# Order of loads, a third output accumulator and new biases in a planned attention and gated-layer kernel

## The chip, the cores and the metric

The kernel runs on one core of a Trainium2 chip. The metric is the time of one execution in device microseconds; of several runs the median is given. The core has five engines that run side by side and wait for each other by semaphores: TensorE (PE, matrix products and transposes), VectorE (DVE), ScalarE (ACT), GpSimd (POOL) and SyncE (SP). In this kernel POOL and SP also issue nearly all transfers: POOL those that change the type from fp32 to bf16, SP those that transpose and the stores of the result.

## The reference

```python
# attention: 8 batches, 8 heads, 576 tokens, 64 columns; heads 0-3 plain, heads 4-7 dilated
scores = matmul(q, k^T) / 8
mask_plain = (rel >= 0) & (rel < 32)
mask_dil   = (rel >= 0) & (rel < 128) & (rel % 4 == 0)
x = softmax(where(mask, scores, -1e9)) @ v        # -> 4608 tokens x 512
# gated layer
h = x @ w_in                                      # 512 -> 2048
g = h * (1 / (1 + exp(-beta * h)))
out = g @ w_out                                   # 2048 -> 512, fp32
```

## The kernel before

All products are done in bf16. The work has two halves that are woven into each other.

**Attention**, per batch of 576 tokens. For heads 0 to 3 (the plain ones) keys are taken in blocks of 96 queries by 128 keys; for heads 4 to 7 (the dilated ones) the tokens are split by their remainder modulo 4 into four sets of 144, of which 128 are done as one block and the last 16 as a "tail". Steps by their names in the planner's lists: K and Q steps transpose keys and queries on PE (lines 474, 484) and copy them out of the accumulators; S are scores (688 dilated, 716 and 752 plain), T the tail's scores (657); each is followed by an exponential on ACT (624) and a multiplication by a 0/1 mask on DVE or POOL (628). V are the products with the values (793 dilated, 809 plain), U the tail's (778), each followed by a division by the row sum on DVE (643, 644). X and Y turn the result into xT, the transposed input of the gated layer (831, 846, 861).

Batches 0 to 2 (DIRECT = 3) load keys and queries to the buffers `st` by `direct_qk` and transpose them on PE. Batches 3 to 7 copy them to DRAM in bf16 by `cast` (POOL's queue) and read them back by transposing loads, `crossbar` (SP's queue, line 465). From batch 2 on (BY_DMA = 2) the result also goes to xT through DRAM and a transposing load (`back_dma`, lines 511 to 538), on SP's queue too. Values are loaded by `direct_vp` (plain, with a halo copied after the load) and by `direct_vd`, which makes three loads: one of the dilated values (line 439, later spread into `vd`) and two of the tail's values `vt_` (line 443).

**The gated layer** has nine tiles of 512 tokens. `slot_h` (line 892) makes one of 16 slots of 128 columns of h by four matmuls, then a tanh on ACT (901) and the gate on DVE (906). `block` makes one of four blocks of 128 rows of the output by 16 matmuls in four parts (927), scales it on ACT or DVE (942, 944) and stores it from SP (947). A part needs only four of the gated slots and its share of w_out; w_out comes in two loads, of which each serves two parts. The first four slots of the first tile (APART = 4) do the dilated half of x first, the plain half after it. Tile t needs attention of batch t and a part of the one before.

**The order** is written by a planner. Every step is a `plan.op` with the engines that can do it, an estimated time, its dependences and a due number `vt`. `Plan.run` keeps its own clock: of the steps that are ready it looks on each engine at those whose start, plus the step's bias, lies within NEAR (40 to 60 ns) of the earliest one, and takes the one with the smallest `vt`. The bias is `NUDGE[n]` in nanoseconds, where n counts the steps in the order in which they are made. So changing `vt` moves a step among others that are ready at the same time, and a bias makes a step look earlier or later than it is. For loads the planner keeps a clock for each queue, with an estimated rate and a latency, and lets at most eight be under way on one queue. Accumulator banks are taken by kinds with a limit each (CAPS): "o" is the kind of the output blocks of all tiles but the last, "h" of the slots, "s", "w", "a" of the attention, and there are eight banks in all. Where PE would stand idle in the plan before 80 us, the planner puts in a filler, a product of zeros (line 1040).

Due numbers of the loads: batch 0's keys and queries -9 to -8.97, its dilated values -8.5, its tail values (-8.5 + 1.255 + .001) -7.244, its plain values -8.4; w_in -7.3 to -7.28; the second batch's rows -7.25 to -7.22 and its values -7.2 to -7.19; w_out -7.2 and -7.19. From the fourth batch on, the loads of batch b are released together by a small copy on POOL (`t_pace`, line 1006), which waits until the work has come far enough; after it stand, by due number, the dilated key cast (b - 2), the dilated query cast (+.01), the plain key cast (+.02), the dilated and tail values (+.02 to +.022), the plain query cast (+.03) and the plain values (+.03).

## Time and profile before

| | before |
|---|---|
| median of 5 runs | 302.44 us (301.38 to 303.53) |
| the profiled execution | 301.85 us |
| its span, first to last instruction | 300.1 us |
| granted clock of TensorE, mean | 1.000 |
| busy share PE / DVE / ACT / POOL | 97% / 61% / 57% / 30% |
| matmuls of 512 columns with w_in (L892) | 550 recorded, 134.5 us |
| the same with w_out (L927) | 540 recorded, 134.1 us |
| fillers (L1040) | 65, the last at 45.0 us |
| transfers on POOL's queue | 18.58 MB, 59.2% of the span of the 16 DMA engines |
| transfers on the queues of SP and ACT | 22.95 MB, 37.4% |

The span is what the profile covers; the time of an execution is about 1.7 us longer. Times inside the profile count from the span's start. A row of the timeline gives the start, the length from the first start to the last end, the engine, the line, what is done (output <- inputs), how many instructions the row joins, and in brackets how long the engine sat idle and what ended that. Ends of matmuls are modelled, since they overlap, so the cost of a row is best read from its start to the next row's start. A POOL row of a transfer is the issue alone. A few per cent of the matmuls have no record.

### The profile page before, as it was taken

To read this page: it belongs to the slowest core of one execution; us is meant where nothing else is said; L and a number is where in the kernel's file an instruction comes from. 1 tells how busy PE (TensorE), PEld (TensorE's weight loads), DVE (VectorE), ACT (ScalarE), POOL (GpSimd) and SP (SyncE) were. 2 spreads that over 40 slices of the span, in tenths; PEclk is the share of its full clock that TensorE was granted. 3 is DMA by queue.
4 is the path that set the end of the run, shared out by engine and by line. 5 is a ranking of instruction groups with operands and counts; after the bars stand their busy time and mean duration, and the time that the engine had idled before them with its cause. 6 is when DMAs were issued, how large, how long until landed. Compare 5 with 4: busy or idle time off the path is not lost.

```text
span 300.1 us, 6040 instructions
## 1 busy us (share of the span) xinstructions
PE 292.6 (97%) x2304; PEld 150.2 (50%) x2342; DVE 184.3 (61%) x415; ACT 171.5 (57%) x311; POOL 90.6 (30%) x130
## 2 busy tenths in 40 slices
PE   7999999999999999999999999999999999999995
PEld 4765556445554445445444544455444444444454
DVE  4769778798858736886477745685781543443300
ACT  3868873867447644765585546764852654555311
POOL 8997363762155204600733065110000000000000
PEclk9999999999999999999999999999999999999999
DMA  7999999699979998999899979996024000100122
GB/s 164 189 210 203 206 190 205 96 174 192 215 152 176 155 146 212 180 151 222 146 191 154 195 158 174 164 202 156 0 75 115 36 36 35 37 35 35 60 82 70
DMA packets 111248, 41.98 MB, mean 140 GB/s; under 512 B 87620, under 2 KB 104596, under 8 KB 111220
## 3 DMA queue, kind: packets, MB, share of 16 engines
q0 software_dynamic: 60336, 18.58, 59.2%
q1 hardware_dynamic: 50740, 22.95, 37.4%
q8 instruction: 18, 0.29, 0.4%
q10 hardware_dynamic: 144, 0.07, 0.1%
q14 instruction: 10, 0.08, 0.1%
HBM read 37.76 MB, written 18.87 MB: 189 GB/s over the span
## 4 chain that ended last, share of the span: by engine, by line
PE 87%; DMA 8%; issue 1%; DVE 1%; POOL 1%; ACT 0%; DVEq 0%; POOLq 0%
PE bank L927 38%; PE bank L892 37%; DMA vp<-in_v_dram 7%; DMA st<-in_q_dram 2%; PE bank L1040 2%; PE bank L809 2%; PE bank L793 1%; PE bank L688 1%; PE bank L716 1%; PE bank L474 1%; PE bank L484 1%; PE bank L778 1%; PE bank L752 1%; PE bank L861 1%; ACT pt L624 0%
## 5 line engine op out<-in xcount | busy, mean ns | idle before, releaser
L901 ACT ACTIVATE tnh<-bank,beta_half 128x512 bf16<-128x512 f32 x144 | 98.1, 690 | 71.1 <-PE bank L892 64.2
L927 PE MATMUL bank<-w_out_bf,g 128*128 128x512 bf16 (+2 forms) x588 | 137.3, 367 | 1.4 <-issue 0.6
L906 DVE SCALAR_TENSOR_TENSOR g<-tnh,bank 128x512 bf16<-128x512 bf16 x144 | 97.2, 685 | 66.4 <-ACT tnh L901 65.8
L892 PE MATMUL bank<-xT,w_in_bf 128*128 128x512 bf16 (+1 forms) x566 | 136.1, 376 | 0.9
L892 PEld LDWEIGHTS <-w_in_bf 128*128 128x128 bf16 x584 | 55.4, 98 | 61.5
L927 PEld LDWEIGHTS <-g 128*128 128x128 bf16 x608 | 54.9, 98 | 56.2
L942 ACT ACTIVATE osb<-bank 128x512 f32<-128x512 f32 (+1 forms) x34 | 20.0, 590 | 31.6 <-PE bank L927 30.6
L624 ACT ACTIVATE pt<-bank 128x384 bf16<-128x384 f32 (+1 forms) x54 | 20.4, 463 | 5.3 <-PE bank L716 3.2
L624 ACT ACTIVATE ptd<-bank 128x512 bf16<-128x512 f32 x32 | 16.8, 603 | 3.7 <-PE bank L688 3.7
L644 DVE TENSOR_TENSOR xsp<-bank,rcp 96x384 bf16<-96x384 f32 x32 | 17.7, 554 | 1.1
L628 DVE TENSOR_TENSOR pt<-pt,mask_n 128x384 bf16<-128x384 bf16 (+1 forms) x39 | 13.4, 361 | 7.0 <-ACT pt L624 6.5
L643 DVE RECIPROCAL rcp<-bank 96x6 f32<-96x6 f32 (+2 forms) x72 | 12.9, 179 | 6.2 <-PE bank L809 3.0
L1006 POOL COPY pace<-xT 1x2 bf16<-1x2 bf16 x4 | 0.7, 176 | 50.1 <-DMA xT<-x 50.1
L399 POOL DMA_DIRECT2D vp<-in_v_dram x9 | 15.2, 1694 | 1.2 <-DMA vp<-in_v_dram 1.2
L644 DVE TENSOR_TENSOR xdm<-bank,rcp 128x256 bf16<-128x256 f32 x32 | 13.6, 424 | 1.1
L399 POOL DMA_DIRECT2D s<-in_q_dram x10 | 13.6, 1357 | 0.0
L628 DVE TENSOR_TENSOR ptd<-ptd,mask_d 128x512 bf16<-128x512 bf16 x27 | 10.8, 422 | 4.5 <-ACT ptd L624 3.8
L399 POOL DMA_DIRECT2D vt<-in_v_dram x16 | 13.3, 1000 | 0.0
L1040 PE MATMUL bank<-zero 128*128 128x256 bf16 x65 | 11.0, 314 | 1.1 <-DVE warm L307 1.1
L399 POOL DMA_DIRECT2D s<-in_k_dram x10 | 11.1, 1105 | 1.5 <-issue 1.1
L809 PEld LDWEIGHTS <-pt 128*128 128x128 bf16 x192 | 8.9, 97 | 5.1 <-issue 0.3
L944 DVE TENSOR_SCALAR osb<-bank 128x512 f32<-128x512 f32 (+2 forms) x4 | 2.1, 525 | 14.0 <-PE bank L927 14.0
(111 smaller groups left out, 184.3 us busy)
## 6 DMA issues: line engine op xcount, KB each, us to landing
out_dram<-osb SPq DMA_DIRECT2D x35, 256.0 KB, 2.6
s<-in_k_dram POOLq DMA_DIRECT2D x10, 288.0 KB, 7.2
s<-in_q_dram POOLq DMA_DIRECT2D x10, 288.0 KB, 9.5
w_out_bf<-in_moe_w_out_dram POOLq DMA_DIRECT2D x2, 1024.0 KB, 16.1
vp<-in_v_dram POOLq DMA_DIRECT2D x7, 288.0 KB, 15.8
st<-in_q_dram POOLq DMA_DIRECT2D x6, 288.0 KB, 12.6
x<-xsp SPq DMA_DIRECT2D x12, 144.0 KB
st<-in_k_dram POOLq DMA_DIRECT2D x5, 288.0 KB, 14.3
```

The source lines that it names most:

```text
L399: {"POOL": nc.gpsimd, "SP": nc.sync}[queue].dma_start(out=out, in_=in_)
L624: nc.scalar.activation(out=w(), in_=sc(), func=ACT.Exp, scale=SCALE)
L628: E[e].tensor_tensor(out=w(), in0=w(), in1=m(), op=ALU.mult)
L643: nc.vector.reciprocal(out=r, in_=p[..., D])
L644: nc.vector.tensor_tensor(out=dst, in0=p[..., 0:D], in1=r.unsqueeze(len(p.shape) - 1).to_broadcast(list(p.shape[:-1]) + [D]), op=ALU.mult)
L809: nc.tensor.matmul(pv[:, a, h2, :], lhsT=lhs, rhs=vp[kv][:, (2 * x + h2) * NI + 3 * j + a, 0:D + 1], start=True, stop=True)
L892: nc.tensor.matmul(bank(g)[:, a:z], lhsT=w_in_bf[:, kt, fb * P:(fb + 1) * P], rhs=xT[:, kt, xo + a:xo + z], start=(i == 0 and kt == kts[0] ...
L901: nc.scalar.activation(out=th[:, 0:n], in_=bank(g)[:, 0:n], func=ACT.Tanh, scale=beta_half[:, fb:fb + 1])
L906: nc.vector.scalar_tensor_tensor(out=g_t[t % 2][:, fb, c0:c0 + n], in0=th[:, 0:n], scalar=1.0, in1=bank(g)[:, 0:n], op0=ALU.add, op1=ALU.mult)
L927: nc.tensor.matmul(bank(g)[:, lo:hi], lhsT=g_t[t % 2][:, fb, tb * P:(tb + 1) * P], rhs=w_out_bf[:, fb, lo:hi], start=(fb == 0), stop=(fb = ...
L942: nc.scalar.mul(out=ob[:, lo:hi], in_=bank(g)[:, lo:hi], mul=0.5)
L1040: nc.tensor.matmul(BANKS[b][:, 0:256], lhsT=zero[:, 0:P], rhs=zero[:], start=True, stop=True)
```

## The change

It has five parts.

1. `direct_vd` of batch 0 gets -8.985 in place of -8.5, so its dilated values stand between the dilated queries (-8.99) and the plain keys (-8.98). The offset of its tail loads grows from 1.255 to 1.74, so that these stay where they were, at -7.244.
2. Both loads of w_out get -7.27 and -7.26: behind w_in, ahead of all rows of the second batch.
3. From the fourth batch on, the plain casts get .03 more (+.05 and +.06), so that they stand behind the dilated, tail and plain values.
4. The limit for kind "o" goes from 2 to 3 accumulators.
5. The table of biases is replaced: 29 entries between step 10 and step 1158 before, with sizes from 60 to 900; the new ones begin at step 48 and have sizes from 60 to 2500.

```diff
-    CAPS = {"h": 3, "p": 4, "o": 2, "z": 4, "a": 8, "s": 5, "w": 6}
+    CAPS = {"h": 3, "p": 4, "o": 3, "z": 4, "a": 8, "s": 5, "w": 6}
     SWITCH = 95
-    NUDGE = {10: 900, 16: -150, 32: -150, 34: 400, 40: -900, 65: -150, 99: -150, 121: -900, 159: -400,
...
+    NUDGE = {48: -900, 51: 150, 55: 150, 56: -150, 57: 400, 62: -2500, 63: -400, 70: -900, 73: 150,
+        75: -900, 78: 2500, 86: -400, 94: -150, 101: -2500, 118: 150, 126: -2500, 132: 900,
...
+        754: -2500, 767: 900, 774: -150, 926: -400, 941: -900, 1102: -900, 1119: -400, 1284: -60}
...
-            out.append(load("POOL", (vt_[b % 2][:, c, :, 0:D], src), list(tdeps), vt + (1.255 if b == 0 else .02 if b < DIRECT else 0) + .001 + .001 * c, 96, .2, lat=1100 if b < DIRECT else 4000))
+            out.append(load("POOL", (vt_[b % 2][:, c, :, 0:D], src), list(tdeps), vt + (1.7399999999999993 if b == 0 else .02 if b < DIRECT else 0) + .001 + .001 * c, 96, .2, lat=1100 if b < DIRECT else 4000))
...
-    ld[0]["vd"] = direct_vd(0, [], -8.5, [fill3])
+    ld[0]["vd"] = direct_vd(0, [], -8.985, [fill3])
...
-                 [], -7.2 + .01 * n, 2048, .41)
+                 [], -7.27 + .01 * n, 2048, .41)
         w_out_ld[2 * n] = w_out_ld[2 * n + 1] = o
...
-                c = cast(b, z, h0, [go], b - 2 + .01 * n)
+                c = cast(b, z, h0, [go], b - 2 + .01 * n + (0 if h0 else .03))
```

## The prediction

> **What bounds the kernel now.** I read the page's busy shares first, then its forty slices, then the costliest groups, and last the timeline of PE alone. The first two show one full engine:

> ```profile
> span 300.1 us, 6040 instructions
> PE 292.6 (97%) x2304; PEld 150.2 (50%) x2342; DVE 184.3 (61%) x415; ACT 171.5 (57%) x311; POOL 90.6 (30%) x130
> ...
> PE   7999999999999999999999999999999999999995
> ...
> PEclk9999999999999999999999999999999999999999
> DMA  7999999699979998999899979996024000100122
> ...
> L1040 PE MATMUL bank<-zero 128*128 128x256 bf16 x65 | 11.0, 314 | 1.1 <-DVE warm L307 1.1
> ```

> PE is full from the second slice to the last but one, always at the full granted clock; nothing else is over 61%. A 512-column matmul takes 0.216 us of it (0.86 us for four in the chain). So time goes away only where PE is busy with something useless, and it is added only where PE runs dry. The useless work is named in the last line: 65 fillers on zeros (L1040), which the planner emits where its own clock finds PE without work. The timeline of PE says when:

> ```profile
> 25.04 0.82 PE L1040 MATMUL bank<-zero 128*128 128x256 bf16 x6
> 25.69 1.03 PE L892 MATMUL bank<-xT,w_in_bf 128*128 128x512 bf16 x3
> ...
> 35.11 1.16 PE L1040 MATMUL bank<-zero 128*128 128x256 bf16 x9
> 36.20 0.43 PE L752 MATMUL bank<-qT,kT 64*128 64x96 bf16 x12
> 36.56 0.28 PE L1040 MATMUL bank<-zero 128*128 128x256 bf16 x1
> 36.68 1.89 PE L927 MATMUL bank<-w_out_bf,g 128*128 128x512 bf16 x7
> ...
> 44.99 0.27 PE L1040 MATMUL bank<-zero 128*128 128x256 bf16 x1
> 45.10 1.03 PE L927 MATMUL bank<-w_out_bf,g 128*128 128x512 bf16 x4
> ...
> 53.21 2.98 PE L892 MATMUL bank<-xT,w_in_bf 128*128 128x512 bf16 x12
> ```

> From start to start, the fillers after 26 us cost 36.20-35.11 = 1.09, 36.68-36.56 = 0.12 and 45.10-44.99 = 0.11: **1.32 us**. Those at 25.04 cost 0.65. All 48 others lie before 18.2 us, where the first product with w_in starts. After 45 us there are none, and PE's rows follow each other to the end: nothing downstream offers more than fractions.

> The break at 35 us ends in the first product with w_out (L927). Its transfers, from the timeline of POOL and from the view of that tile:

> ```profile
> 19.25 0.90 POOL L399 DMA_DIRECT2D w_out_bf<-in_moe_w_out_dram  x1
> 25.50 0.88 POOL L399 DMA_DIRECT2D w_out_bf<-in_moe_w_out_dram  x1 [0.40 <-DMA st<-in_k_dram]
> ```
> ```profile
> DMA to landing us min/median/max: 15.9/16.1/16.3
> ```

> They land at about 35.2 and 41.8. By then the 16 slots of the first token tile are through, so w_out is what is late.

> **The output weights first.** No transfer is added. One of 1,024 KB (1.05 MB) at the 206 GB/s of the window 30 to 37.5 takes 5.1 us. The last w_in lands at 10.96 + 12.8 = 23.8 (third issue in POOL's row at 9.45; page, DMA issues). With both parts of w_out next, they land at 28.9 and 34.0 instead of 35.2 and 41.8. PE's next work after 25.7 us is eight slots of the first tile, 32 x 0.216 = 6.9 us, to 32.6. From 28.9 on, first halves of output blocks can be taken too: with three accumulators 3 x 2 parts x 0.86 = 5.2 us, with two 3.4 us. Either bridges 32.6 to 34.0, when the second half is there; the third accumulator makes it safe. So I let the 1.32 us go. It cannot be more than 1.32 + 0.65; it is nothing if the planner finds other gaps.

> The 0.65 us at 25.04 I keep: there PE waits for the last part of w_in, which stands where it did. This is also why an earlier start would not help: before 25.7 PE can only do the first eight slots and batch 0's attention, and it had done both.

> The cost is that the second batch's rows, which lay ahead of one or both parts, go behind. The first key rows landed when the wait at 25.50 ended; they now land at 34.0 + 1.4 = 35.4 (288 KB at 206 GB/s), some 10 us later. The tail values of batch 0 move along; their product (PE at 27.93) is needed only by the second tile. The group's end does not move: the same bytes are in front of it, and batch 1's plain values (POOL idle 1.20 at 44.33 for a vp landing) arrive near 43.5 as before. On POOL each issue blocks until the eighth before it has landed; batch 1's dilated values then issue at 28.9, its plain ones at 34.0, and batch 2's keys after batch 1's last key transposes, near 40 instead of 29 to 32. The queue still holds batch 1's values until 44, so this is hidden by 4 us; if that cover goes, batch 2's rows slide by what is missing.

> What batch 1's attention loses is room. DVE and ACT now have this to do:

> ```profile
> 26.00:36.00 10.00, 9.90 (x161) 5.83 (x161) 8.20 (x16) 8.33 (x17) 5.23 (x7) 1.00 1.26 206
> 36.00:53.20 17.20, 16.88 (x243) 9.92 (x244) 13.67 (x36) 10.44 (x25) 8.30 (x13) 1.00 1.57 201
> 53.20:72.00 18.80, 18.64 (x164) 9.36 (x155) 15.57 (x37) 13.90 (x28) 11.89 (x15) 1.00 1.33 139
> ```

> (Columns after the length: busy PE, weight loads, DVE, ACT, POOL; clock; DMA share; GB/s.) In the first two rows DVE and ACT do 40.6 us. Eight slots take 8 x (0.69 + 0.69) = 11.0 of it; the remaining 29.6, nearly all of batches 1 and 2, must now start after about 36.6 (35.4 and the transposes). Up to 53.2 that is 16.6 us on each engine, 33.2 in all: 89% busy. In the third row, the fullest stretch, they reach 29.5/37.6 = 78%; at that rate the work ends at 36.6 + 29.6/(2 x 0.78) = 55.6. What covers it is output work: the L927 rows from 36.7 to 53.2 hold 41 matmuls of the tile's 64, so some 23, or 5.0 us, are left. PE, 1.3 us ahead, therefore has work until 53.2 - 1.3 + 5.0 = 56.9. The chain by itself is no longer: the last query rows at 40.2, transposed, copied, scored, exponentiated and masked in about 5 us by the rows from 34.7 to 38.6, meet the values at 46, where L809 starts now (45.96). I take 0. The bounds are 0 and a stall of 3.5 us (if the pair reached only 65%: 36.6 + 22.8 = 59.4, against 56.9, and a last link of 1 us).

> The TensorE clock stays at 1.00 in every row above, and there is no idle stretch of PE that could tell what one costs. [...]

> **The other parts.** Batch 0's dilated values move ahead of its plain keys and queries: 256 KB at the 189 GB/s of that stretch, so those come 1.4 us later and the values 2.9 us earlier. The dilated halves of the first slots can begin at the first w_in, which removes fillers before 18 us, but the wall at 25.7 stands: 0, between -2.2 (the wall is partly the planner's own estimate: w_in landed at 23.8, and 0.3 more) and +1.4. Mask, identity and issue order on POOL change without bias by some 0.3 us each, under the queue's backlog: 0.

> From the fourth batch on, the plain casts go behind all values. POOL issues the same eight transfers; the plain query cast lands later by the plain values' time, and the plain values earlier by the two casts. SP, which issues the transposing loads in order, then meets batch b's plain ones later. The tightest case:

> ```profile
> 107.90 3.27 SPq L465 DMA_TRANSPOSE qT<-s  x1
> ...
> 111.32 0.48 DVE L248 COPY vp<-vp 32x1280 bf16<-32x1280 bf16 x1 [1.17 <-DMA vp<-in_v_dram]
> ...
> 116.49 0.69 PE L716 MATMUL bank<-qT,kT 64*128 64x96 bf16 x24
> ```

> The transposing load would start about 111.3 - 107.9 = 3.4 us later and the scores near 120. PE does w_out and w_in products in that time, and the back transposes of batch 3, which stood in SP's queue behind this load, come sooner. In the other batches the scores (L716 at 84.8, 154.9, 190.6, 206.5) start 9 us and more after that load's issue. I take 0; bounds -0.5 and +2.

> Biases: they reorder about equal work on a full PE. Rows 'issue' ahead of L927 sum to 0.6 us on the page; -0.6 to +1.5, I take 0.

> **Sum.** -1.3 us. The profiled execution took 301.85 with a span of 300.1, so 298.8 and 300.5; against the median of the runs (302.44, from 301.38 to 303.53) it is 301.1. I forecast between the two: **300.8**.

> **Rivals.**
> - *The start gets shorter too* (the wall at 25.7 is the planner's; -2 to -4.2, 298.2 to 300.4, say 299.2). For: w_in landed at 23.8 and PE took it at 25.69. Against: its place in the queue is unchanged. Chance 0.2.
> - *The fillers only move* (to the wall, or to 50 to 56 us before the second tile): 301.7 to 303.1, say 302.4. For: the planner's estimate makes them. Chance 0.17.
> - *DVE and ACT become the bound from 36 to 57 us*: the second batch's transposed rows are late, PE has used up the first tile's output blocks, and waits. From 56.9 on every microsecond is paid; 3.5 of stall less 1.3 gives +2.2, 304.2 and up to 306 where batch 2 slides as well. For: 89% needed against 78% seen. Against: 5 us of output work in reserve. Chance 0.16.
> - The forecast itself, 299.9 to 301.7: 0.47.

> Differences under 0.5% (1.5 us) can't be told from none here: 300.9 and 304.0 are the limits. Of the forecast's 0.47, 0.30 lies below 300.9. Faster 0.30 + 0.20 = 0.50; the same 0.17 + 0.17 = 0.34; slower 0.16. The range leaves out most of the slower case and the best end of the first rival: 298.5 to 304.0.

> **What would show it.** Right: both w_out issues ahead of all second-batch rows, landing near 29 and 34; no L1040 row after 26 us; the first L927 row at 29 to 34; the second tile's L892 stream starting near 52; DVE and ACT nearly full from 37 to 54. Wrong: L1040 rows or PE idle for ACT or DVE between 46 and 58, PE idle anywhere after 100 us for a qT load, or a first w_in product well before 18.2 together with the slots done before 25.

## The result and the profile after

The changed kernel takes 303.34 us (median of 48 executions, 301.66 to 306.34), the kernel before beside it 302.03 us (88 executions, 300.87 to 303.53). The ratio is 1.0037, with a 95% interval from 1.0027 to 1.0048; a ratio here is one of means, without executions over 1.5% above the fastest of their kernel (one of the 48). So the change made the kernel slower by 0.37%, some 1.1 us, or 1.3 us by the medians, where I had forecast 1.6 us less than the median of 302.44 then shown; it is less than a few runs could tell from none, but these many do. The times alone held a clue. They lie in three groups with gaps between them: 18 from 301.7 to 302.8, 26 from 303.1 to 304.3, and 4 from 305.8 to 306.3. The kernel before has one broad group.

The first profile of the changed kernel fell into the lowest group (302.58 us) and shows almost nothing wrong. Lines are shifted by 8: L892, L927 and L1040 are now L900, L935 and L1048. The page:

```profile
span 300.6 us, 6020 instructions
PE 291.7 (97%) x2294; PEld 149.4 (50%) x2333; DVE 183.9 (61%) x418; ACT 169.9 (57%) x304; POOL 95.2 (32%) x134
...
L1048 PE MATMUL bank<-zero 128*128 128x256 bf16 x56 | 10.8, 328 | 1.3 <-DVE warm L315 1.1
```

There are nine fillers fewer, yet their busy time is 10.8 us against 11.0, and seven still stand after 26 us, where none was expected. The timeline of PE says where they are now:

```profile
24.13 0.71 PE L1048 MATMUL bank<-zero 128*128 128x256 bf16 x5
25.64 2.15 PE L900 MATMUL bank<-xT,w_in_bf 128*128 128x512 bf16 x9 [0.80 <-DMA w_in_bf<-in_moe_w_in_dram]
...
30.09 0.38 PE L1048 MATMUL bank<-zero 128*128 128x256 bf16 x2
...
31.17 1.03 PE L935 MATMUL bank<-w_out_bf,g 128*128 128x512 bf16 x4
...
57.92 2.33 PE L900 MATMUL bank<-xT,w_in_bf 128*128 128x512 bf16 x9
```

The first product with w_out comes at 31.17 instead of 36.68, and after 30.30 there is no filler at all. The second tile's stream, however, begins at 57.92 instead of 53.21, while the first tile's output blocks fill PE up to there. Summed from start to next start, the fillers compare like this:

| stretch, us | before | changed, first profile | changed, three more profiles |
|---|---|---|---|
| 0 to 6.6 | 4.28 | 5.29 | 5.07 to 5.21 |
| 6.6 to 18.2 | 3.99 | 3.20 | 3.20 |
| 18.2 to 26 | 0.66 | 1.51 | 0.60 to 0.61 |
| from 26 | 1.32 | 0.77 | 0.96 |
| all | 10.24 | 10.77 | 9.84 to 9.98 |

The 1.51 of the first profile holds the wait of 0.80 us for w_in. So the fillers mostly moved: 0.4 to 0.6 us went after 26 us, and the sum ends 0.3 to 0.4 us below that of before, or 0.5 us above it with the wait. Against that stands a new wait: near 6.3 us PE stands dry for 0.55 to 1.29 us in these four profiles (under 0.4 in the kernel before), for the constant `add_d` that POOL makes for the scores. POOL ends it at 6.37 us in the first profile instead of 5.37, behind the moved load of batch 0's dilated values. That goes far to explain why a good execution is no better than the kernel before. It does not explain the two upper groups.

A second profiled execution did (run "again" below, the same kernel, 305.88 us). SP's timeline of it, ahead of the place where PE runs dry:

```profile
159.45 1.97 SPq L519 DMA_DIRECT2D x<-xsp  x2
168.33 1.28 SPq L473 DMA_TRANSPOSE kT<-s  x1
...
170.32 1.31 SPq L473 DMA_TRANSPOSE qT<-s  x1
171.73 3.26 SPq L546 DMA_TRANSPOSE xT<-x  x2
```

and PE's timeline in the same execution:

```profile
173.62 1.03 PE L935 MATMUL bank<-w_out_bf,g 128*128 128x512 bf16 x4
177.03 5.31 PE L900 MATMUL bank<-xT,w_in_bf 128*128 128x512 bf16 x16 [2.38 <-DMA xT<-x]
```

SP has issued the writes of batch 5's result to DRAM at 159.45 and 161.01; by the trace they have landed at 167.85 and 168.76, and the back transposes (xT, L546) could follow. But the two transposing loads of batch 6's plain keys and queries (kT, qT, L473) stand ahead of them in SP's order, and these wait for casts that land at 168.28 and 170.09. The back transposes go out at 171.73 and 173.22, the first of them 3.9 us after its source was there. The last output block ready is used up at 174.65, the data of the first back transpose land at 176.98, and PE stands idle for 2.38 us. Then 16 matmuls take 5.31 us, where the first profile has 3.62 for the same 16:

```profile
175.43 3.62 PE L900 MATMUL bank<-xT,w_in_bf 128*128 128x512 bf16 x16
```

The views by stretch of the stalled execution say why; their columns are those of the prediction:

```profile
177.00:180.00 3.00, 2.97 (x9) 1.13 (x10) 0.69 (x1) 0.69 (x1) 1.72 (x4) 0.59 0.66 135
180.00:181.00 1.00, 1.00 (x4) 0.38 (x3) 0.06 (x1) 0.69 (x1) 1.00 (x3) 0.51 0.57 41
181.00:184.00 3.00, 3.00 (x15) 1.35 (x14) 2.01 (x3) 1.97 (x3) 3.00 (x5) 1.00 1.03 181
```

The granted clock fell to half, from 177.57 us for 3.41 us by the trace, and PE lost another 1.7 us. In the kernel before, SP has the same instructions in this order:

```profile
157.26 2.63 SPq L465 DMA_TRANSPOSE kT<-s  x1
...
162.97 2.32 SPq L465 DMA_TRANSPOSE qT<-s  x1
165.38 0.53 SPq L511 DMA_DIRECT2D x<-xsp  x1
168.78 1.29 SPq L538 DMA_TRANSPOSE xT<-x  x1
...
171.30 1.30 SPq L538 DMA_TRANSPOSE xT<-x  x1
```

and PE this row:

```profile
174.12 2.75 PE L892 MATMUL bank<-xT,w_in_bf 128*128 128x512 bf16 x11
```

There qT is also ahead of xT, but it is gone by 165.3, before the result is written: the two writes land at 168.76 and 171.29, and each back transpose follows its write at once. What PE takes at 174.12, with no wait, is the data of the first one, which land at 172.33. So this place had 1.8 us to spare before the change, and the change took that away.

Where do the late casts come from? In the first profile after, batch 6's transfers are released at 147.64, 3.3 us later than before (144.35). The plain key cast lands 19.1 us after the release and the query cast 21.9 us (before: 10.8 and 18.6), because all the values are now issued ahead of both. So kT is later by 8.3 us and qT by 3.3 us through the third part, and both by another 3.3 us through the release. The release waits for the second back transpose of batch 4, which lands at 147.01 instead of 143.73. That one too stands behind batch 5's plain loads, issued at 136.46 and 139.89 when their casts have landed (before: 127.08 and 133.09). So part of the later release comes by the same way, one batch earlier; how much is not shown. With 3.3 us alone the query cast would have landed near 166.3 us (estimate, 162.96 + 3.3), ahead of the writes that the back transposes wait for. By that it took both delays.

### The profile page after: what moved, and what is told of

Same layout as the page of the kernel before. It is cut to its first block, busy times and chain, and to the rows that moved or that the text cites. A ratio compares the mean times of both kernels' runs of the same rounds, so it can differ in the third digit from the quotient of the medians.

```text
span 300.6 us, 6020 instructions
## 1 busy us (share of the span) xinstructions
PE 291.7 (97%) x2294; PEld 149.4 (50%) x2333; DVE 183.9 (61%) x418; ACT 169.9 (57%) x304; POOL 95.2 (32%) x134
## 4 chain that ended last, share of the span: by engine, by line
PE 89%; DMA 4%; POOL 3%; issue 2%; DVE 0%; ACT 0%; POOLq 0%; DVEq 0%
PE bank L935 41%; PE bank L900 39%; DMA w_in_bf<-in_moe_w_in_dram 4%; PE bank L817 2%; PE bank L696 1%; PE bank L801 1%; PE bank L724 1%; PE bank L482 1%; PE bank L786 1%; PE bank L492 1%; POOL st L407 0%; POOL w_in_bf L407 0%; PE bank L760 0%; PE bank L665 0%; POOL vp L407 0%
## 5 line engine op out<-in xcount | busy, mean ns | idle before, releaser
L935 PE MATMUL bank<-w_out_bf,g 128*128 128x512 bf16 (+2 forms) x581 | 137.8, 367 | 1.8 <-issue 0.6
L900 PE MATMUL bank<-xT,w_in_bf 128*128 128x512 bf16 (+1 forms) x572 | 136.7, 376 | 1.5 <-DMA w_in_bf<-in_moe_w_in_dram 0.8
L900 PEld LDWEIGHTS <-w_in_bf 128*128 128x128 bf16 x584 | 55.8, 98 | 63.7 <-DMA w_in_bf<-in_moe_w_in_dram 1.1
L935 PEld LDWEIGHTS <-g 128*128 128x128 bf16 x608 | 54.5, 98 | 55.4
L950 ACT ACTIVATE osb<-bank 128x512 f32<-128x512 f32 (+2 forms) x30 | 17.4, 581 | 22.0 <-PE bank L935 21.7
L632 ACT ACTIVATE pt<-bank 128x384 bf16<-128x384 f32 (+1 forms) x54 | 21.1, 461 | 10.8 <-PE bank L724 7.6
L651 DVE RECIPROCAL rcp<-bank 128x4 f32<-128x4 f32 (+2 forms) x72 | 12.9, 179 | 9.0 <-PE bank L801 3.6
L636 POOL TENSOR_TENSOR pt<-pt,mask_n 128x288 bf16<-128x288 bf16 (+1 forms) x10 | 7.4, 762 | 32.2 <-ACT pt L632 16.4
L636 DVE TENSOR_TENSOR pt<-pt,mask_n 128x384 bf16<-128x384 bf16 (+1 forms) x36 | 11.7, 352 | 9.1 <-ACT pt L632 8.9
L952 DVE TENSOR_SCALAR osb<-bank 128x512 f32<-128x512 f32 (+1 forms) x8 | 5.1, 636 | 13.7 <-PE bank L935 13.7
L1048 PE MATMUL bank<-zero 128*128 128x256 bf16 x56 | 10.8, 328 | 1.3 <-DVE warm L315 1.1
L407 POOL DMA_DIRECT2D vp<-in_v_dram x9 | 10.2, 1130 | 4.1 <-DMA w_out_bf<-in_moe_w_out_dram 4.1
## 6 DMA issues: line engine op xcount, KB each, us to landing
s<-in_q_dram POOLq DMA_DIRECT2D x10, 288.0 KB, 10.2
```

What stands on the lines that cost most here:

```text
L407: {"POOL": nc.gpsimd, "SP": nc.sync}[queue].dma_start(out=out, in_=in_)
L632: nc.scalar.activation(out=w(), in_=sc(), func=ACT.Exp, scale=SCALE)
L636: E[e].tensor_tensor(out=w(), in0=w(), in1=m(), op=ALU.mult)
L651: nc.vector.reciprocal(out=r, in_=p[..., D])
L900: nc.tensor.matmul(bank(g)[:, a:z], lhsT=w_in_bf[:, kt, fb * P:(fb + 1) * P], rhs=xT[:, kt, xo + a:xo + z], start=(i == 0 and kt == kts[0] ...
L935: nc.tensor.matmul(bank(g)[:, lo:hi], lhsT=g_t[t % 2][:, fb, tb * P:(tb + 1) * P], rhs=w_out_bf[:, fb, lo:hi], start=(fb == 0), stop=(fb = ...
```

## The experiments

I went in with theory A (the start: w_in lands just when it is needed), theory B (the crowded second batch) and theory C (the clock is at half for longer at the start). Theory D, the queue of SP in batch 6, was formed on the second profile; F is what A to C become beside it. In the later expectations "rival C" means something else, full transfer engines, and R and S are named where they come up.

**The changed kernel again.** No edit.

> The changed kernel once more, for a second profile and its spread beside the variants. Theory A (the start): the 48 times lie in groups near 302.1, 303.6 and 306.1 us because the last part of w_in now lands just when PE needs it (25.59 against 25.64 us; before it landed 23.8 and was used at 25.69), so that any delay of that transfer goes straight to the end. In a profile whose span is over 301.3 the first product after the wall near 25.6 us then starts up to 1.6 us later, and all else is shifted by that. Theory B (the crowded second batch): the first slots start at 25.6 as in the first profile, and a long span gains its time between 36 and 60 us, where batch 1's attention is crowded. Theory C (the clock): a long span shows the TensorE clock at half for longer at the start (over 5.8 us).

Measured: 303.16 us (301.80 to 306.48), ratio 1.0038 [1.0011, 1.0065]. The profile is the one shown above. It speaks against theory A: w_in's last part lands at 24.47 and is taken at 24.54 without a wait, while the wait of 0.80 us for it, with a landing at 25.59, is in the first profile, of the lowest group.

**The tail mask behind the loads of w_in, in the changed kernel.** One bias is put back; only POOL's order changes, and the last part of w_in lands at 24.33 us. In the first profile of the changed kernel that was 25.59, but in the three others it is 24.47 to 24.65, so the edit moves less than it was meant to.

```diff
-    NUDGE = {48: -900, 51: 150,
+    NUDGE = {10: 900, 48: -900, 51: 150,
```

> The changed kernel with the old bias of step 10 alone (+900): the tail mask goes on POOL behind the issues of w_in instead of between the first and the second. Every other engine keeps its order. Theory A: w_in's second and third parts are issued 1.1 us sooner, the third lands near 24.5 instead of 25.6, the 0.8 us that PE waits there go and the group near 303.6 becomes rare: 0.8 to 1.5 us faster than the changed kernel, equal to the kernel before or up to 0.4 us faster. Theory B: w_in may land earlier, but the time stays within 0.3 us of the changed kernel's.

Measured: 302.99 us (301.70 to 306.51), ratio 1.0019 [0.9999, 1.0038]. The groups stay: five executions from 301.7 to 302.6, six from 303.0 to 304.4, one at 306.5. Nothing changes that can be told apart. With w_in landing early and without a wait in all three profiles from the upper groups (again, again_2, again_3), theory A falls.

**The reverse, in the kernel before.** Its bias on step 10 is taken away, so the tail mask goes between the loads of w_in; again only POOL's order changes, and w_in's last part lands at 24.10 instead of 23.80.

```diff
-    NUDGE = {10: 900, 16: -150,
+    NUDGE = {16: -150,
```

> The kernel before without the bias of step 10: the tail mask goes ahead on POOL, between issues of w_in, and no other engine changes its order. Theory A: w_in's last part lands about 1 us later, at 24.8 instead of 23.8, still ahead of its use at 25.69, so the time stays within 0.5 us, slower if anything (up to 0.5 us) because the reserve is down from 1.9 to 0.9 us. Theory B: no change.

Measured: 301.37 us (300.92 to 302.87), ratio 0.9981 [0.9964, 0.9998], the wrong way for A. It was run again later (the expectation calls the tail mask the dilated one):

> The kernel before without its bias on step 10, once more (only POOL's order changes: the dilated mask is built among the loads of the input weights). If its first ratio, 0.9981, stands: 0.996 to 0.9995. If it was chance: 0.999 to 1.002.

Measured: 302.25 us (301.26 to 303.03), ratio 1.0010 [0.9992, 1.0028]. The gain did not stand, and the order at the start is worth nothing measurable in either kernel.

**The old biases with the four other parts.** The table of the kernel before in the changed kernel.

> The changed kernel with the old table of biases: its four other parts without the fifth. Theory A: the mask and the identity return behind and ahead of w_in, so w_in lands 1 us or more sooner; as fast as the kernel before or up to 1.5 us faster. Theory B: the second batch's rows are as late as in the changed kernel, so it is 1 us or more slower than the kernel before. Against both: the old biases were numbered for another order, and PE may run dry anywhere, which would show as idle time of PE after 60 us.

Measured: 310.59 us (308.56 to 310.87), ratio 1.0257 [1.0231, 1.0283]. The fillers after 26 us take 4.9 us instead of 0.8 to 1.0, and PE stands dry before 97.5, 120.9 and 222.5 us for 0.9, 1.7 and 0.9 us. The new biases are worth 7 us to the new order.

**The two plain loads behind the back transposes, from the fifth batch on.** The plan stays. When it comes to such a load before batch b - 1 has its two back transposes, the load is put aside and issued right behind them. Only SP's order changes.

```diff
+        if not h0 and b > DIRECT:
+            o.after = b - 1
```

> The changed kernel with one thing altered: on SP the transposing loads of plain queries and keys of the fifth batch on are issued behind the back transposes of the batch before them, instead of ahead of them; every other engine's order is as in the changed kernel. Theory D (the later plain casts make those loads wait in SP's queue, the back transposes stand behind them, the stored output blocks run out, and in many executions PE stands dry near 174 us or at the same place in another batch, up to 2.4 us and then 3.4 us at half clock): no execution near 306, no group at 303 to 304.4, median 301.7 to 302.3, ratio to before 0.998 to 1.001, PE never idle for 0.5 us after 26 us. Theory F (the stall at 174 us is rare and by itself; the 303.6 group is made elsewhere, at the start or in the second batch): only the times at 306 go, median still near 303, ratio near 1.003. Rival: the plain loads that are now late make the batch's own score work late, ratio above 1.004.

Measured: 302.29 us (301.64 to 309.60), ratio 1.0003 [0.9977, 1.0029] over the eight executions below 307. Seven executions lie from 301.6 to 302.5, none from 303.0 to 304.4, but five from 304.9 to 309.6. The profile, from the lower group, has no PE wait of 0.5 us after 26 us. D's group is gone and something new has come. In the batches on either side, the plain keys and queries now stand last, the queries 3.6 to 4.7 us ahead of their scores.

**The same in batch 6 alone.**

```diff
-        if not h0 and b > DIRECT:
+        if not h0 and b == 6:
```

> The changed kernel with batch 6's two plain transposing loads alone issued on SP behind batch 5's back transposes; every other order on every engine stays. It is the earlier experiment cut down to the batch in which the stall was seen. Theory D: no stall near 174 us, no execution at 303.0 to 304.4, median 301.7 to 302.3; and the executions at 304.9 to 309.6 that the wider experiment had in 5 of 12 are gone, since they came from the other batches' loads, whose data the scores need 3 to 5 us after they landed there. If they stay, this batch's own loads or a transfer nobody reordered make them. Rival C (full DMA engines): executions near 303.5 and 306 stay.

Measured: 301.95 us, and all 11 executions between 301.61 and 302.67; ratio 1.0016 [1.0007, 1.0026]. SP's timeline, with lines shifted once more (kT and qT are L490, xT is L566):

```profile
159.41 2.12 SPq L539 DMA_DIRECT2D x<-xsp  x2
162.55 0.36 SPq L976 DMA_DIRECT2D out_dram<-osb  x1
167.97 3.04 SPq L566 DMA_TRANSPOSE xT<-x  x2
171.11 1.30 SPq L490 DMA_TRANSPOSE kT<-s  x1
172.51 1.32 SPq L490 DMA_TRANSPOSE qT<-s  x1
```

and PE's at the place of the stall:

```profile
173.86 1.03 PE L956 MATMUL bank<-w_out_bf,g 128*128 128x512 bf16 x4
174.73 3.62 PE L921 MATMUL bank<-xT,w_in_bf 128*128 128x512 bf16 x16
```

The casts land at 167.92 and 170.99 here, the query cast later than in the stalled execution, and it does no harm. The upper groups are gone, and so are the executions above 304.9 of the wider edit, which therefore came from the other batches' loads. Which one of those loads it was is not shown. SP is idle from 162.9 to 167.97, and what the first back transpose waits for there is its write, issued at 159.41 and landed at 167.91. So transfers set that time, as in the stalled execution (167.85), and the order added 3.9 us to it there. Of that wait rival C may have a share; that busy DMA engines make these writes take over 8 us is not shown, for the kernel before has a lower DMA share from 165 to 170 (1.14 in the view by stretch, against 1.64 here) and its first write takes 7.4 us.

To see whether anything else was lost, the changed kernel and this version were run side by side on one chip.

> The changed kernel once more, beside the next run on the same chip. Theory D alone: 302 to 303.4 median, with executions near 302.1, near 303.5 and near 306. Nothing new is expected of it; it is the measure for the next one.

> The changed kernel with batch 6's two plain transposing loads behind batch 5's back transposes, once more, beside the changed kernel. Theory D alone (all the loss is the stall near 174 us): no execution above 303.0, median 1.0 to 1.5 us below the changed kernel's median on this chip, and level with the kernel before, ratio 0.998 to 1.0015. Theory S (something at the start is lost as well, some 0.5 us): the same step down from the changed kernel, but ratio 1.001 to 1.003 to the kernel before.

Measured: the changed kernel 303.54 us (301.94 to 306.27), ratio 1.0058 [1.0034, 1.0083]; with the two loads moved 302.01 us (301.66 to 302.36), ratio 0.9996 [0.9981, 1.0011]. The places of two instructions on one queue are worth 1.5 us. Here that is the whole loss and theory S is not needed; the earlier run of the same version, 1.0016 [1.0007, 1.0026], leaves some 0.5 us. Whether anything of that size is lost besides stays open.

**A second profile of the changed kernel between the groups.**

> The changed kernel once more, for a second profile and more executions. Theory D: again three groups of times near 302.1, 303.6 and 306.1; the profile's time says which: near 303.6 or 306 it holds a PE wait of 0.5 us or more for an xT transpose after 100 us, near 302.1 it holds none. Theory F: near 303.6 the profile holds no such wait, and the loss stands before 60 us.

Measured: 303.35 us (301.66 to 303.72), ratio 1.0023 [1.0002, 1.0043]. The profiled execution took 303.45 us and has one PE wait of 0.5 us after 26 us, 1.39 us for xT before 176.28; the profiled execution of the run just before (again_3) took 303.73 us and waits 1.63 us at the same place:

```profile
176.28 3.63 PE L900 MATMUL bank<-xT,w_in_bf 128*128 128x512 bf16 x16 [1.39 <-DMA xT<-x]
176.56 3.63 PE L900 MATMUL bank<-xT,w_in_bf 128*128 128x512 bf16 x16 [1.63 <-DMA xT<-x]
```

In neither did the clock fall there. So each group has its cause in a profile: no wait near 302; 1.4 to 1.6 us of wait near 303.5; 2.4 us of wait and 1.7 us of half clock near 306. Of all 84 executions of the changed kernel 28, 47 and 9 are in the three groups, and none lies between 304.3 and 305.6. The mean clock, which is on record for every execution, bears this out: 0.993 or 0.994 in all nine of the highest group, as 3.41 us at half clock would give, and at least 0.998 in the 75 others. The kernel before is not quite free of such a fall: beside the variants two of its 96 executions took 306.3 and 306.6 us with a clock of 0.994. Theory C finds nothing: the first record of full clock begins at 5.76 us in the first profile (ahead of it fillers start 0.21 us apart, later 0.11) and at 6.90, 4.10 and 5.38 us in the three from the upper groups.

**The third part alone in the kernel before**, with the old biases.

> The kernel before with only the third part, the values' casts ahead of the plain ones from the fourth batch on, and the old biases. Theory D: the plain transposing loads' casts land 4 to 8 us later and the back transposes behind them too, so PE stands dry in some batches: 302.8 to 306, ratio 1.002 to 1.013, with a PE wait on an xT transpose in the profile. Theory F (the start and the second batch make the loss): level with before, ratio 0.999 to 1.001.

Measured: 306.36 us (304.25 to 307.51), ratio 1.0125 [1.0090, 1.0161]. After 26 us PE waits once, 3.4 us before 113.61, for the second back transpose of batch 3, issued at 103.92, and the clock is at half for 3.41 us behind it. No load that waits for its cast holds this one; ahead of it SP has only the issues of the first (3.74 us) and of the dilated queries (3.49 us). Its own data take 9.65 us to land, while the values and both plain casts, issued from 89.5 to 93.9, land between 99.2 and 113.5. So here the transfers keep PE waiting, as rival C has it. That the third part made them slow is not shown: in the kernel before the first back transpose of this batch takes 10.2 us (100.77 to 110.95), and nothing waits for it.

**The second part alone in the kernel before**, with the old biases.

> The kernel before with only the second part: both output-weight loads ahead of the second batch's rows. Theory D: no back transpose is touched, so after 60 us nothing changes; fillers after 26 us go down from 1.32 us and the second batch comes later: 301.0 to 302.5, ratio 0.996 to 1.002. Theory F: the second batch's rows are late, PE stalls or fillers between 35 and 60 us: ratio 1.003 or more.

Measured: 311.73 us (308.46 to 313.64), ratio 1.0286 [1.0237, 1.0335], a miss for both theories in size. Fillers take 13.94 us instead of 10.24, 5.0 of them after 26 us, and PE stands dry for xT for 3.4 us before 123.61. Every later step is planned anew and the old biases don't fit.

**The third part taken back in batch 6 alone, in POOL's order only.**

> The changed kernel with the third part taken back in one batch alone, batch 6, and in nothing but the order of POOL's issues: the plain keys' cast stands ahead of the values' loads and the plain queries' cast ahead of the padded values', as in the kernel before; every order on PE, DVE, ACT and SP stays. Theory D (those casts land at 166.7 and 169.5 us, SP waits for them, and batch 5's back transposes, issued at 170.9 and 172.4, stand behind): both casts land by 163, the second back transpose is issued by 170, PE has no wait of 0.5 us after 100 us, nothing near 303.6 or 306: median 301.7 to 302.3, ratio 0.998 to 1.001. Rival R (the values, now later, are what is late: their copies, at 157.1 and 164.4 us in the changed kernel, move behind 165 and something waits for them): ratio stays at 1.002 or more with a wait behind a values' load. Rival C (the DMA engines are full in that stretch, so the back transposes' own data come late whatever the order): PE still waits for xT near 174 in some executions, ratio 1.002 or more.

Measured: 311.61 us (310.61 to 311.97), ratio 1.0329 [1.0311, 1.0346]. Rival R, and strongly. DVE's timeline and, in the next fence, PE's (L269 is the halo copy of the padded values, L948 w_out, L913 w_in):

```profile
162.80 0.69 DVE L927 SCALAR_TENSOR_TENSOR g<-tnh,bank 128x512 bf16<-128x512 bf16 x1 [0.45 <-ACT tnh L922]
171.17 0.48 DVE L269 COPY vp<-vp 32x1280 bf16<-32x1280 bf16 x1 [7.68 <-DMA vp<-in_v_dram]
```
```profile
164.41 1.03 PE L948 MATMUL bank<-w_out_bf,g 128*128 128x512 bf16 x4
172.43 5.28 PE L913 MATMUL bank<-xT,w_in_bf 128*128 128x512 bf16 x12 [6.99 <-DVE g L927]
```

The changed kernel's order has the halo copy at 164.4 in DVE's queue, because the values are due by then. With the padded values back at 171.08 the copy blocks DVE for 7.7 us, every gate behind it waits, and PE with them, for 6.99 us; by the view by stretch the clock is at 0.50 from 168 to 176 us. The third part is therefore built into the orders of the other engines, and this run says nothing for or against D.

**The second part taken back** (w_out's due numbers -7.2 again), planned anew.

> The changed kernel without the second part: the output weights are loaded behind the second batch's first rows again, as before; third accumulator, values' order and the new biases stay. It is planned anew, so later orders move as well. Theory D says nothing of the start; the prediction's own step gave this part 1.32 us of fillers after 26 us: by it the fillers after 26 us rise from 0.77 to about 1.3 to 2 us and the time is 0.5 to 1.5 us above the changed kernel's stall-free 302.1, plus what the biases, made for another order, lose. If the fillers only move, their sum over the span stays within 0.3 us of 10.8 us. If the biases lose as in the kernel with the old ones: 305 or more, with PE waits after 60 us.

Measured: 314.37 us (313.42 to 316.43), ratio 1.0435 [1.0401, 1.0468]. Fillers after 26 us rise to 1.83 us and their sum to 11.27; the rest is PE waiting for DVE and ACT, 0.4 to 2.0 us at a time, from 80 to 132 us, and half clock for 6.83 us from 129.13.

**The third accumulator taken back** ("o" 2), planned anew.

> The changed kernel with two output accumulators instead of three; all else stays, planned anew. If the third accumulator is what lets first output work start while second-batch banks are held, as the prediction had it: PE waits or fillers between 30 and 60 us grow by 0.5 to 2 us, 302.5 to 304.5. If it is worth nothing: 301.7 to 303.6 as the changed kernel. If the biases, made for the other order, lose: 305 or more, with PE waits after 60 us.

Measured: 308.15 us (307.12 to 308.94), ratio 1.0217 [1.0196, 1.0238]. Between 26 and 60 us nothing changes, no PE wait of 0.5 us and 0.96 us of fillers; the loss is later, with 0.64 us of fillers near 77 and 81 us and above all 2.36 us of waiting for xT before 126.56. These last two and the two single parts in the kernel before price a part together with biases made for another order, so none of the four is the price of the part.

## Why the prediction was wrong, step by step

- **What bounds the kernel** was right. PE is full in both kernels, and all that was lost is time in which PE stood dry, or ran at half clock just after.
- **Plain casts behind the values, priced at 0 with bounds -0.5 and +2: the step that failed.** The step said that PE has other work in the meantime and that "the back transposes of batch 3, which stood in SP's queue behind this load, come sooner". They came later: at 112.62 and 114.12 in the first profile after, instead of 100.77 and 112.33, still behind qT. The delay of qT was sized well (3.4 us; batch 6 shows 3.3). In batch 4 itself, where 3.3 us came out too (111.24 instead of 107.90), that is luck: its cast landed 19.8 us after the release against 20.0 before, and the release was 5.4 us later. Above all I looked at one batch only, and from the consumer's side, where the scores have microseconds to spare. I did not ask who stands behind qT in SP's queue when the result of the batch before is already written. In batch 6 it is the back transposes, whose data had 1.8 us to spare. The price of that order on SP is 1.5 us on the median (303.54 less 302.01) and up to some 4 us in single executions. That the third part alone would have cost it is not shown: half of the delay of qT there came with the later release.
- **Output weights first, priced at -1.32: the mechanism was right, the size was not.** The two parts landed at 30.6 and 35.7 in the first profile and about 1 us earlier in the others (forecast 28.9 and 34.0), the first L935 row stood at 31.17, and the fillers after 26 us fell from 1.32 to between 0.77 and 0.96. But the plan has 0.8 to 1.0 us more of them before 6.6 us and 0.8 less from there to 18.2. The sum of the fillers fell by 0.3 to 0.4 us in most profiles. The version without the stall measures the whole: ratios 0.9996 and 1.0016 in its two runs, not -1.3 us. That was the second rival, "the fillers only move" (302.4), to which I had given 0.17.
- **The wall at 25.7 us at 0** was right in the sum: w_in's last part was taken at 25.64 in the first profile and at 24.54 to 24.81 in the three others, as it landed, and no time follows that.
- **The crowded second batch at 0, bounds 0 to 3.5** was right. The second tile came 5.9 us later than I said, at 57.92, and nothing waited: the output blocks were the reserve I had counted. DVE and ACT did 12.47 + 11.57 = 24.0 us of work from 36 to 53.2, 70% of the two, not 89%, since POOL took 11.3 us and more of the batch was done later.
- **Batch 0's dilated values, mask and identity at 0**: the whole time shows no loss, but it did not go "under the queue's backlog". PE waits 0.55 to 1.29 us near 6.3 us for `add_d`. (The values' 2.9 us should be 3.1, two loads of 288 KB at the 189 GB/s named there; nothing in the sum rests on it.)
- **The third accumulator "makes it safe"**: with two there was no loss before 60 us, as the sum of the step had it.
- **Biases at 0, -0.6 to +1.5** were right only for the parts taken together. Without the new ones the change costs 8.4 us (1.0257), so they are worth 7 us, and "about equal work on a full PE" was no way to bound them.
- **The price of a stall.** The prediction counts a stall at its own length ("3.5 of stall less 1.3 gives +2.2"). That holds for the stalls of 1.4 and 1.6 us and is 1.7 us short for the one of 2.4 us, behind which the clock was at half for 3.41 us.

The signs of a wrong prediction came near the place where it failed, with "PE idle anywhere after 100 us for a qT load", but with no price; PE was idle for xT, which stood behind the qT load. The time lies within the range; the sign of the change does not lie where most of the chance was.

## What to carry to other kernels

When a load is made later, its own consumer is the smaller question. List what stands behind it in the queue that issues it, for every batch and not only the one with the tightest consumer, and compare the moment at which each of those could go with the moment at which the load will let it go. When the times of one program fall in separate groups, a single profile shows only one of them: take profiles until each group has one. And one part of an order that was fitted as a whole can't be priced by taking it out alone: here a copy in DVE's queue, and the biases, depended on it.
